# Folding the query weights in 32 by 32 array tiles, in two halves around the last key burst

## The chip, the cores and the metric

The kernel runs on one core of a Trainium2 chip. The metric is the device time of one execution in microseconds; the median of three runs of the kernel before is 507.56 us (507.46 to 507.66). Everything below comes from one further execution that was profiled.

## The reference

The kernel computes a gated mix of two branches over S = 2048 rows of width D = 512, all in float32:

```python
x = A_x
g = _sigmoid((x * gate_w).sum(-1, keepdims=True))
a = _A_ref(x, A_wqkv, A_w_phi, A_wo)      # linear attention, 32 heads of 16
b = _B_ref(x, B_w1, B_b1, B_w2, B_b2)     # relu(x @ w1 + b1)**2 @ w2 + b2, F = 1792
return g * a + (1 - g) * b
```

In branch A, `q`, `k` and `v` are `x @ wqkv`. Each head's `q` and `k` are multiplied by a 16 by 16 matrix (`w_phi`), and go through a softmax of both signs. The keys' features and `v` give a small matrix per head, `kv`, and a sum `z`; the queries' features are multiplied with them.

Since `q` is only ever used as `q @ w_phi`, the kernel multiplies the weights first: the query weights "folded" are `wq @ w_phi` head by head, a 512 by 512 matrix. This fold is what is changed here.

## The kernel before, in words

The contraction index of every product is cut into four chunks of 128 (`k` = 0 to 3), rows into blocks of 512, and the feed-forward width into 14 chunks. To keep float32 accuracy on TensorE, each operand is split into a high part (rounded, written by ScalarE: `activation ... Copy`, L63) and a low part (the rest, written by VectorE: a subtraction, L66), and a product is three matmuls (high by high, high by low, low by high: L76, L77, L78).

The program is one long list of work items. For each there is an `up` product (into a PSUM bank named `u`, read by ScalarE's ReLU at L421, then squared and split into `hh` and `hl`) and, two items later, a `down` product (into banks `d`). In this document u28, u29 and u30 are the up products with `w1` chunks 7, 8 and 9 around the change, one after the other. Attention work is hung between them at numbered slots by the calls of `at(slot, f)`; a scheduler then sets each engine's order by these and by priorities (`tc.high_priority`), and each engine runs its instructions strictly in the order built.

What lies around the change:

- The first seven chunks of the feed-forward run over all rows with the keys' and values' projections; the last key burst (`kvps`, L323) closes `kv`. VectorE then copies `kvps` out (L751), transposes it (L760) and writes `kvb` (L764), and SyncE writes `zrow` and loads `z` from it.
- The key weights are folded early, at 26 us, by `tiles_fold`: 64 matmul calls (128 records in the trace, two a call) of 32 by 32 weights and 128 columns, spread over all sixteen 32 by 32 tiles of the array and over four PSUM banks, with the roles of the operands swapped, so that VectorE's block transposition (L194) turns the result.
- The query weights are folded at slots 53 to 56 by `do_fold`: for each `k` four 128 by 128 products into one bank (`foldq`, L152), split into `wqh`, `wql` by ScalarE and VectorE straight from PSUM.
- At slot 56.5 the first projection of queries (`q`) needs all four `wqh`, `wql`.
- Three PSUM banks rotate at that time among `u`, `pY` and the folds (`bank`); a fourth joins with `kv_done`.
- Staging tiles `in` (four) hold loaded weights until they are split; a load waits until VectorE has split the tile's last content. `gated` (L445) adds a block's `d` banks into `row` tiles that ScalarE has filled (L893).

The program's functions that the change touches, with the line numbers of the profile:

Of the kernel before, what the change touches and what calls it, by code (L numbers as in the profile page):

```python
# [7 lines left out]
F32 = mybir.dt.float32  # L8
F32R = mybir.dt.float32r
# [6 lines left out]
P = 128  # L16
S, D, H, DH, F = 2048, 512, 32, 16, 1792
NK = D // P
# [10 lines left out]
AHEAD = 150  # L29
# [5 lines left out]
def tile_gated_mix(ctx: ExitStack, tc: tile.TileContext, xT, xn, wqT, wkT, wphi, wv, wo, w1, b1, w2, b2, gw, out):  # L35
    nc = tc.nc
# [4 lines left out]
    wpool = pool("wpool", 1)  # L41
    fpool = pool("fpool", NFH)
    work = pool("work", 2)
# [4 lines left out]
    banks = [ps_a, ps_b, ps_e, ps_f]  # L48
    def used(p):
        banks.remove(p)  # L50
        banks.append(p)

    def bank(name):
        p = banks[0]
        used(p)
        return p.tile([P, 512], F32, tag="s", name=name)
# [4 lines left out]
    def split(src, hi, lo, ehi, elo):  # L61
        if ehi is nc.scalar:
            i = nc.scalar.activation(hi, src, AF.Copy)  # L63
        else:
            i = ehi.tensor_copy(hi, src)
        st["lo"] = elo.tensor_tensor(lo, src, hi.bitcast(F32), ALU.subtract)  # L66
        return i
# [52 lines left out]
    st, up_w, down_w = {}, {}, {}  # L120
# [24 lines left out]
            nc.sync.dma_start(t[g + 1], wT[:, g, :])  # L145
        return t

    def fold(loaded, nm, k):
        wph, *t = loaded
        ps = bank(f"fold{nm}{k}")  # L150
        for g in range(NK):
            nc.tensor.matmul(ps[:, g * P:(g + 1) * P], t[g][:, k * P:(k + 1) * P], wph[:, g * P:(g + 1) * P],  # L152
                             start=True, stop=True)
        hi = wpool.tile([P, 512], F32R, tag=f"wah{k}", name=f"w{nm}h{k}")
        lo = wpool.tile([P, 512], F32R, tag=f"wal{k}", name=f"w{nm}l{k}")
        with tc.high_priority(offset=AHEAD):
            split(ps, hi, lo, nc.scalar, nc.vector)
        return hi, lo

    def both(t):  # L160
        return t[:, :512], t[:, 512:]

    def joint_start(loaded):
# [6 lines left out]
        for k in (0, 2, 1, 3):  # L170
            r = st["tmp"][k // 2] if k % 2 else work.tile([P, 2 * D], F32, tag="e", name=f"raw{k}", bufs=2)
            st["raw"][k] = r
            st["wv"] = nc.sync.dma_start(two(r)[:, :, 256:], two(wv[k * P:(k + 1) * P, :]))

    def tiles_fold(loaded):
        wph, *t = loaded
        pss = [bank(f"fold{r}") for r in range(4)]

        def mm(g, r, c):
            rows, cols = slice(32 * r, 32 * r + 32), slice(32 * c, 32 * c + 32)  # L180
            return nc.tensor.matmul(pss[r][cols, g * P:(g + 1) * P],
                                    wph[rows, g * P + 32 * r:g * P + 32 * r + 32],
                                    t[g][rows, :].rearrange("p (k c q) -> p k c q", c=4, q=32)[:, :, c, :],
                                    start=True, stop=True, skip_group_check=True)

        last = None
        for x in [(g, r, c) for g in range(NK) for c in range(4) for r in range(4)]:
            with tc.issue_after(last.ins) if last else nullcontext():
                last = mm(*x)
        for half in range(2):  # L190
            tb = work.tile([P, 2, 4, NK, 32], F32, tag="tb", name="turned", bufs=2)
            for r in range(2):
                with tc.high_priority(offset=AHEAD):
                    st["turned"] = nc.vector.transpose(tb[:, r].rearrange("p g k q -> p (g k q)"), pss[2 * half + r])  # L194
            for k in range(NK):
                dst = st["raw"][k].rearrange("p (h z g r f) -> p h z g r f", h=2, z=2, g=2, r=4)
                for h in range(2):
                    nc.scalar.activation(dst[:, h, 0, :, 2 * half:2 * half + 2],
                                         tb[:, :, 2 * h:2 * h + 2, k].rearrange("p r g q -> p g r q"), AF.Copy)

    def operand(i, j, src, slot=None, ehi=None, elo=None):
        if i in HELD:
# [116 lines left out]
    def kv_chunk(first, last, kvps, phi, v):  # L319
        for g in range(NG):  # L320
            for j in range(4):
                h = NG * j + g
                mm = nc.tensor.matmul(kvps[32 * j:32 * j + VW, 32 * g:32 * g + 32], v[:, h * VW:(h + 1) * VW],  # L323
                                      phi[:, 32 * h:32 * h + 32], start=(first and g == 0), stop=last,
                                      skip_group_check=True)
        return mm
# [129 lines left out]
    def do_wT(wT):  # L456
        st["wT"] = load_fold(wT)

    def do_fold(nm, k):
        with tc.issue_after(st["up"].ins):  # L460
            st["wa", nm, k] = fold(st["wT"], nm, k)
        if k == NK - 1:
            st["wa"] = [st["wa", nm, i] for i in range(NK)]
            if nm == "k":
                banks.pop()

    def do_joint(j, piece):
        if (j, piece) == (0, 0):
            joint_start(st["wT"])
            with tc.issue_after(st["up"].ins):  # L470
                tiles_fold(st["wT"])
        with tc.issue_after(st["up"].ins):
            joint(j, piece)
        if (j, piece) == (1, 0):
            banks.remove(ps_b)
# [121 lines left out]
    LASTP = len(ROWS) - 1  # L597
# [59 lines left out]
    def pair_steps(p, s):  # L657
        b, c = ROWS[p]
        n, m = b * NC + c, b * NC + c + 2
        v = {}  # L660
# [49 lines left out]
        def kv():  # L710
            if p == 0:
                st["kv"] = ps_b.tile([P, 2 * P], F32, tag="s", name="kvps")
            later = kv_chunk(p == 0, False, st["kv"], v["phi", m], v["v", m])
            with tc.issue_after(later.ins):
                kv_chunk(False, p == LASTP, st["kv"], v["phi", n], v["v", n])

        at(s - 2 - (p > 0), sums_load, p)
        if p == 0:
# [7 lines left out]
        at(s + 3, phi, n)  # L726
        at(s + 4, phi, m)
        at(s + 7.5 + (p == LASTP) / 2, kv)

    def do_q(b, n, c):  # L730
# [16 lines left out]
    def kv_done():  # L747
        kvps, kvs = st["kv"], st["kvs"]
        for j in range(4):
            s = slice(32 * j, 32 * j + VW)  # L750
            nc.vector.tensor_copy(kvs[s, :], kvps[s, :])  # L751
        nc.sync.dma_start(zrow.rearrange("(j x) -> j x", j=4), kvs[DH::32, :])
        for half in range(2):
            z = hold.tile([P, H * VW], F32, tag="vz", name=f"z{half}")[:, :D]
            nc.sync.dma_start(z, zrow[half * D:(half + 1) * D].partition_broadcast(P))
            zbc.append(z.rearrange("p (h f) -> p h f", f=DH))
        banks.append(ps_b)
# [27 lines left out]
    def at(slot, f, *a):  # L785
        steps.setdefault(int(2 * slot) / 2, []).append(lambda: f(*a))
# [10 lines left out]
    for b in range(NB):  # L797
        for c in range(NC):
            s = b * SL + 2.5 * c - 1 if b > 1 else 17.5 + c / 2 if b else max(5.5, 3.5 + 2 * c)
# [5 lines left out]
        s, late = ((4, 2), (19.5, 1), (22, 2.5), (36, 2))[b]  # L805
# [4 lines left out]
        pair_steps(p, 14 + 4.5 * p)  # L810
    base = (NB - 1) * SL
    at(49, do_wT, wqT)
    for k in range(NK):
        at(53 + k, do_fold, "q", k)
    for k in range(NK):
        at(base + 8.5 + k, wo_load, k)
        at(base + 10 + k, wo_split, k)
# [10 lines left out]
    for p in range(NB * NC // 2):  # L828
        n, s = 2 * p, 56.5 + 6 * p
        q, late = divmod(n, NC)[0], p == NB * NC // 2 - 1  # L830
# [13 lines left out]
    hid, last = {}, len(work_list) - 1  # L844
# [25 lines left out]
    for t, (sw, b, i) in enumerate(work_list):  # L870
# [17 lines left out]
        for c in range(NC):  # L888
            n = b * NC + c
# [62 lines left out]
```

## Time and profile before

| | |
|---|---|
| median of 3 runs | 507.56 us |
| the profiled execution, its time | 507.18 us |
| the profiled execution, first to last instruction | 505.4 us |
| TensorE busy | 500.7 us, 99% |
| VectorE busy | 407.0 us, 81% |
| ScalarE busy | 256.6 us, 51% |
| granted TensorE clock, mean | 0.999 of full |

The execution's time is 1.78 us longer than the span of its instructions. Matmuls overlap, so that each is listed longer than the distance to the next one; what a stretch of TensorE costs is read from start to start. In the timeline one row is one instruction or several alike, with their start, their duration and, in brackets, how long the engine was idle before and what released it.

### The profile page before, as it was taken

The numbers are of one execution on the slowest core, as the hardware profiler recorded it, in microseconds if no ns is written. First come the engines' busy times: TensorE is split into PE (matmuls) and PEld (weight loads), VectorE is DVE, ScalarE is ACT, GpSimd is POOL, SyncE is SP. The second block draws the span as 40 slices with busy tenths as digits, with TensorE's granted clock in tenths as the row PEclk, the third lists the DMA queues.
The fourth block names the chain that finished last, engine by engine and source line by source line (L and its number), as shares of the span: only waits on it lengthen the run. The fifth ranks groups of instructions, "written<-read, shape, count | busy, mean of one in ns | idle before, by whom it ended". The sixth has DMA issues, their size and how long they took to land.

```text
span 505.4 us, 9354 instructions
## 1 busy us (share of the span) xinstructions
PE 500.7 (99%) x3520; PEld 406.1 (80%) x3520; DVE 407.0 (81%) x680; ACT 256.6 (51%) x458; POOL 87.3 (17%) x102
## 2 busy tenths in 40 slices
PE   9999999999999999999999999999999999999997
PEld 5878888788888888888888878788787878788776
DVE  5569957988695979796998989897979796897724
ACT  4887655565253474454674744454455353333540
POOL 1000151204410035000013040212222221112200
PEclk9999999999999999999999999999999999999999
DMA  8858587756854578771265311325112231041112
GB/s 261 291 196 273 198 305 225 237 190 234 285 184 165 183 223 294 265 228 65 83 211 209 98 49 48 99 64 150 49 31 90 71 86 43 8 131 57 38 27 83
DMA packets 45829, 76.13 MB, mean 151 GB/s; under 512 B 6868, under 2 KB 23000, under 8 KB 45784
## 3 DMA queue, kind: packets, MB, share of 16 engines
q1 hardware_dynamic: 36072, 41.78, 26.6%
q10 hardware_dynamic: 6768, 23.79, 13.7%
q0 software_dynamic: 2944, 9.96, 5.5%
q8 instruction: 28, 0.46, 0.4%
q14 instruction: 17, 0.14, 0.1%
HBM read 57.68 MB, written 11.54 MB: 137 GB/s over the span
## 4 chain that ended last, share of the span: by engine, by line
PE 98%; DMA 1%; DVE 0%; issue 0%
PE d L76 10%; PE d L77 10%; PE d L78 10%; PE u L76 10%; PE u L77 9%; PE u L78 9%; PE pX L653 3%; PE q L77 3%; PE att L77 3%; PE att L78 3%; PE att L76 3%; PE q L78 3%; PE q L76 3%; PE pX L655 3%; PE pX L654 3%; PE pY L655 2%
## 5 line engine op out<-in xcount | busy, mean ns | idle before, releaser
L421 ACT ACTIVATE r<-u,b1c 128x512 f32<-128x512 f32 x56 | 38.5, 687 | 122.9 <-PE u L78 121.2
L76 PE MATMUL d<-w2h,hh 128*128 128x512 f32 x222 | 86.9, 391 | 0.0
L77 PE MATMUL d<-w2l,hh 128*128 128x512 f32 x222 | 86.4, 389 | 0.0
L78 PE MATMUL d<-w2h,hl 128*128 128x512 f32 x222 | 86.4, 389 | 0.0
L76 PE MATMUL u<-xh,w1h 128*128 128x512 f32 x212 | 83.6, 394 | 0.0
L77 PE MATMUL u<-xl,w1h 128*128 128x512 f32 x212 | 82.6, 390 | 0.0
L78 PE MATMUL u<-xh,w1l 128*128 128x512 f32 x212 | 82.5, 389 | 0.0
L333 POOL TENSOR_TENSOR ez<-e,z 128x512 f32<-128x512 f32 x32 | 42.9, 1360 | 165.0 <-ACT e L309 165.0
L66 DVE TENSOR_TENSOR hl<-r,hh 128x512 fp32r<-128x512 f32 x56 | 37.8, 676 | 24.3 <-ACT hh L63 24.1
L76 PEld LDWEIGHTS d<-w2h,hh 128*128 128x128 f32 x222 | 41.7, 188 | 9.2 <-issue 0.6
L76 PEld LDWEIGHTS u<-xh,w1h 128*128 128x128 f32 x212 | 39.8, 188 | 11.1 <-issue 2.9
L78 PEld LDWEIGHTS d<-w2h,hl 128*128 128x128 f32 x222 | 41.7, 188 | 8.7
L77 PEld LDWEIGHTS d<-w2l,hh 128*128 128x128 f32 x222 | 41.7, 188 | 8.5
L78 PEld LDWEIGHTS u<-xh,w1l 128*128 128x128 f32 x212 | 39.8, 188 | 8.6 <-DVE w1l L66 0.2
L77 PEld LDWEIGHTS u<-xl,w1h 128*128 128x128 f32 x212 | 39.8, 188 | 7.9
L309 ACT ACTIVATE e<-e 128x1024 f32<-128x1024 f32 x27 | 28.6, 1059 | 26.5 <-DVE e L307 26.1
L291 DVE TENSOR_REDUCE sm<-e 128x64 f32<-128x1024 f32 x27 | 32.8, 1215 | 10.8 <-ACT e L309 10.8
L63 ACT ACTIVATE hh<-r 128x512 fp32r<-128x512 f32 x56 | 35.2, 628 | 1.1
L423 ACT ACTIVATE r<-r 128x512 f32<-128x512 f32 x56 | 34.9, 624 | 0.7
L692 ACT ACTIVATE tmp<-pX 128x512 f32<-128x512 f32 x24 | 14.4, 598 | 30.6 <-PE pX L655 27.0
L374 ACT ACTIVATE phiT<-tb 32x256 f32<-32x256 f32 x64 | 26.4, 412 | 5.8 <-DVE tb L359 4.9
L343 DVE TENSOR_REDUCE dz<-ez 128x64 f32<-128x1024 f32 x16 | 19.4, 1212 | 11.7 <-POOL ez L333 11.7
(182 smaller groups left out, 984.2 us busy)
## 6 DMA issues: line engine op xcount, KB each, us to landing
sloto<-wkeep ACTq DMA_DIRECT2D x30, 512.0 KB, 4.6
in<-in_xT SPq DMA_DIRECT2D x42, 256.0 KB, 4.4
slotez<-wkeep ACTq DMA_DIRECT2D x15, 512.0 KB, 5.0
phiT<-tb SPq DMA_DIRECT2D x192, 32.0 KB, 1.8
in<-in_w SPq DMA_DIRECT2D x23, 256.0 KB, 3.3
part<-row POOLq DMA_DIRECT2D x16, 256.0 KB, 5.5
row<-part SPq DMA_DIRECT2D x16, 256.0 KB, 3.0
out<-row SPq DMA_DIRECT2D x15, 256.0 KB, 2.2
```

Of the source, the lines that this page charges most:

```text
L63: i = nc.scalar.activation(hi, src, AF.Copy)
L66: st["lo"] = elo.tensor_tensor(lo, src, hi.bitcast(F32), ALU.subtract)
L76: nc.tensor.matmul(o, ah[:, sa], bh[:, sb], start=first, stop=False)
L77: nc.tensor.matmul(o, ah[:, sa], bl[:, sb], start=False, stop=False)
L78: return nc.tensor.matmul(o, al[:, sa], bh[:, sb], start=False, stop=last)
L291: nc.vector.tensor_reduce(sm, e3, AX.X, ALU.add)
L309: nc.scalar.activation(ef, ef, AF.Exp)
L333: nc.gpsimd.tensor_tensor(ez[:, hs, :], e3[:, hs, :], zbc[half], ALU.mult)
L374: nc.scalar.activation(dst, src, AF.Copy)
L421: st["relu"] = nc.scalar.activation(r, ps, AF.Relu, bias=b1c[:, fc:fc + 1])
L423: nc.scalar.activation(r, r, AF.Square)
L655: nc.tensor.matmul(ps, l, wh, start=False, stop=j == 1, skip_group_check=True)
```

## The change

The query fold is done as the key fold was: 32 by 32 weights, operands swapped, results turned by VectorE's block transposition out of PSUM into an SBUF tile (`turned`), which is then split. It is done in two halves of 32 matmul calls each (64 products as the trace counts them, two records a call), each on eight array tiles (two row groups by four column groups) and two banks. The first half stands in the middle of u28, before the last key burst, the second in the middle of u29, behind it. Each half fills half of the columns of each `wqh[k]` and `wql[k]`, so there are eight narrower splits where there were four. The splits of the fold no longer have high priority; the transpositions and the copies out of `kvps` now have it.

```diff
-    def fold(loaded, nm, k):
-        wph, *t = loaded
-        ps = bank(f"fold{nm}{k}")
-        for g in range(NK):
-            nc.tensor.matmul(ps[:, g * P:(g + 1) * P], t[g][:, k * P:(k + 1) * P], wph[:, g * P:(g + 1) * P],
-                             start=True, stop=True)
-        hi = wpool.tile([P, 512], F32R, tag=f"wah{k}", name=f"w{nm}h{k}")
-        lo = wpool.tile([P, 512], F32R, tag=f"wal{k}", name=f"w{nm}l{k}")
-        with tc.high_priority(offset=AHEAD):
-            split(ps, hi, lo, nc.scalar, nc.vector)
-        return hi, lo
...
+    def fold_block(loaded, out, g, r, c):
+        wph, *t = loaded
+        rows, cols = slice(32 * r, 32 * r + 32), slice(32 * c, 32 * c + 32)
+        return nc.tensor.matmul(out[cols, g * P:(g + 1) * P], wph[rows, g * P + 32 * r:g * P + 32 * r + 32],
+                                t[g][rows, :].rearrange("p (k c q) -> p k c q", c=4, q=32)[:, :, c, :],
+                                start=True, stop=True, skip_group_check=True)
+
+    def turned(pss, half):
+        tb = work.tile([P, 2, 4, NK, 32], F32, tag="tb", name="turned", bufs=2)
+        for r in range(2):
+            with tc.high_priority(offset=AHEAD):
+                st["turned"] = nc.vector.transpose(tb[:, r].rearrange("p g k q -> p (g k q)"), pss[2 * half + r])
+        return tb
...
+    def query_fold(half):
+        pss = {r: bank(f"fold{r}") for r in (2 * half, 2 * half + 1)}
+        for g, c, r in [(g, c, r) for g in range(NK) for c in range(4) for r in pss]:
+            with tc.issue_after(st["up"].ins):
+                st["up"] = fold_block(st["wT"], pss[r], g, r, c)
+        tb = turned(pss, half)
+        part_ = lambda t: t.rearrange("p (g r f) -> p g r f", g=NK, f=32)[:, :, 2 * half:2 * half + 2, :]
+        for k in range(NK):
+            if not half:
+                st.setdefault("wa", []).append(tuple(
+                    wpool.tile([P, 512], F32R, tag=f"wa{hl}{k}", name=f"wq{hl}{k}") for hl in "hl"))
+            hi, lo = st["wa"][k]
+            split(tb[:, :, :, k].rearrange("p r g q -> p g r q"), part_(hi), part_(lo), nc.scalar, nc.vector)
...
-                kv_chunk(False, p == LASTP, st["kv"], v["phi", n], v["v", n])
+                st["up"] = kv_chunk(False, p == LASTP, st["kv"], v["phi", n], v["v", n])
...
-            nc.vector.tensor_copy(kvs[s, :], kvps[s, :])
+            with tc.high_priority(offset=AHEAD):
+                nc.vector.tensor_copy(kvs[s, :], kvps[s, :])
...
-    for k in range(NK):
-        at(53 + k, do_fold, "q", k)
+    at(52.5, query_fold, 0)
+    at(54.5, query_fold, 1)
```

`tiles_fold` (the key fold) now calls the same two helpers and computes in the same order as before.

The change also moves instructions on the other engines. On VectorE, between the end of the key burst and the first reduction over `q` (`mx`), the order before was (`wql` are the folded query weights' low parts, `row<-d` is `gated`):

```order
L66 TENSOR_TENSOR wol_2995<-in,woh_2994 128x512
L66 TENSOR_TENSOR w1l_3008<-in,w1h_3007 128x512
L66 TENSOR_TENSOR wql_3030<-foldq_3024,wqh_3029 128x512
L66 TENSOR_TENSOR hl<-r,hh 128x512
L66 TENSOR_TENSOR wol_3034<-in,woh_3033 128x512
L445 SCALAR_TENSOR_TENSOR row<-d_2348,rest,row 128x512
L66 TENSOR_TENSOR wql_3084<-foldq_3078,wqh_3083 128x512
L66 TENSOR_TENSOR w2l_3053<-in,w2h_3052 128x512
L445 SCALAR_TENSOR_TENSOR row<-d_2349,rest,row 128x512
L445 SCALAR_TENSOR_TENSOR row<-d_2350,rest,row 128x512
L445 SCALAR_TENSOR_TENSOR row<-d_2351,rest,row 128x512
```

The last low part stood behind one `gated` and ahead of the other three. The same place on VectorE now, from the second half's transpositions to the second half's four low parts:

```order
L174 STREAM_TRANSPOSE turned<-fold_3042 128x512
L174 STREAM_TRANSPOSE turned<-fold_3043 128x512
L66 TENSOR_TENSOR wol_3030<-in,woh_3029 128x512
L66 TENSOR_TENSOR w1l_3088<-in,w1h_3087 128x512
L449 SCALAR_TENSOR_TENSOR row<-d_2348,rest,row 128x512
L449 SCALAR_TENSOR_TENSOR row<-d_2349,rest,row 128x512
L449 SCALAR_TENSOR_TENSOR row<-d_2350,rest,row 128x512
L449 SCALAR_TENSOR_TENSOR row<-d_2351,rest,row 128x512
L66 TENSOR_TENSOR wql_2901<-turned,wqh_2900 128x4x64
L66 TENSOR_TENSOR wql_2905<-turned,wqh_2904 128x4x64
L66 TENSOR_TENSOR wql_2909<-turned,wqh_2908 128x4x64
L66 TENSOR_TENSOR wql_2913<-turned,wqh_2912 128x4x64
```

All four `gated` now stand ahead of the low parts, of which there are four narrow ones here; before, three of the four stood behind the last. Ahead of this piece stand, from the product of the last keys' features (`e<-e,r`) on: two transpositions of the first half, the gate's operations, `w2l`, `wol`, four narrow `wql`, `w1l`, four copies of `kvps`, `hl`, `wol`, `w2l`, the transposition and three of the four copies into `kvb`.

On ScalarE at the same place, before (`r<-u` is the ReLU of u29, `w1h<-in` the high part of a loaded `w1` chunk):

```order
L63 ACTIVATE w2h_2975<-in 128x512
L63 ACTIVATE wqh_2990<-foldq_2985 128x512
L63 ACTIVATE woh_2994<-in 128x512
L421 ACTIVATE r<-u,b1c 128x512
L63 ACTIVATE w1h_3007<-in 128x512
L63 ACTIVATE wqh_3029<-foldq_3024 128x512
```

The ReLU stood ahead of `w1h` and the block's fillings of `row` came later than all of these. On ScalarE at this place now:

```order
L63 ACTIVATE w2h_3019<-in 128x512
L890 ACTIVATE row<-b2b,rest 128x512 x2
L63 ACTIVATE woh_3029<-in 128x512
L63 ACTIVATE w1h_3087<-in 128x512
L890 ACTIVATE row<-b2b,rest 128x512 x2
L425 ACTIVATE r<-u,b1c 128x512
L63 ACTIVATE wqh_2900<-turned 128x4x64
```

The ReLU of u29 now stands behind `w1h` and the four fillings of `row`, and the second half's high parts behind it.

On TensorE at the first projection of queries, before, from the middle of u30:

```order
L78 MATMUL u<-xh_1_2061,w1l_2569 128x512
L76 MATMUL q_3096<-wqh_2890,xh_0_2037 128x512
L77 MATMUL q_3096<-wql_2891,xh_0_2037 128x512
L78 MATMUL q_3096<-wqh_2890,xl_0_2038 128x512
L76 MATMUL q_3096<-wqh_2990,xh_1_2061 128x512
```

The projection ran through from its first matmul. On TensorE at this place now:

```order
L78 MATMUL u<-xh_1_2061,w1l_2569 128x512
L76 MATMUL q_3158<-wqh_2900,xh_0_2037 128x512
L76 MATMUL u<-xh_2_2085,w1h_2568 128x512
L77 MATMUL u<-xl_2_2086,w1h_2568 128x512
L77 MATMUL q_3158<-wql_2901,xh_0_2037 128x512
```

Two matmuls of u30 have moved ahead of the first one that reads `wql`. u30 itself is computed into the bank that u29 used, before and now, so its first matmul waits for u29's ReLU.

## Rows read from the trace of the kernel before

**Rows 1.** The page: the chain that ended last, shares by engine.
```profile
PE 98%; DMA 1%; DVE 0%; issue 0%
```
**Rows 2.** Timeline of TensorE, 244 to 260 us: start, duration, line, names, count.
```profile
244.48 0.39 PE L78 MATMUL u<-xh,w1l 128*128 128x512 f32 x1
244.71 1.05 PE L152 MATMUL foldq<-row 128*128 128x128 f32 x8
...
245.83 0.40 PE L77 MATMUL d<-w2l,hh 128*128 128x512 f32 x1
...
257.03 1.05 PE L152 MATMUL foldq<-row 128*128 128x128 f32 x8
...
259.30 0.39 PE L76 MATMUL q<-wqh,xh 128*128 128x512 f32 x1
```
**Rows 3.** Timeline of TensorE at the key fold.
```profile
26.15 0.39 PE L78 MATMUL d<-w2h,hl 128*128 128x512 f32 x1
...
26.46 1.90 PE L181 MATMUL fold<-row 32*32 32x128 f32 x128
...
28.63 0.40 PE L77 MATMUL d<-w2l,hh 128*128 128x512 f32 x1
```
**Rows 4.** Timeline of TensorE at one numerator burst.
```profile
297.15 0.39 PE L78 MATMUL u<-xh,w1l 128*128 128x512 f32 x1
297.47 1.09 PE L385 MATMUL num<-phiT,kvb 64*32 64x256 f32 x32
...
298.83 0.40 PE L77 MATMUL u<-xl,w1h 128*128 128x512 f32 x1
```
**Rows 5.** Timeline of VectorE, 244 to 261 us.
```profile
244.99 1.21 DVE L314 TENSOR_TENSOR e<-e,r 128x1024 f32<-128x1024 f32 x1
246.12 0.69 DVE L266 SCALAR_TENSOR_TENSOR row<-row,gwb 128x512 f32<-128x512 f32 x1
...
246.73 0.68 DVE L66 TENSOR_TENSOR wql<-foldq,wqh 128x512 fp32r<-128x512 f32 x1
...
249.94 0.68 DVE L66 TENSOR_TENSOR wol<-in,woh 128x512 fp32r<-128x512 f32 x1
250.55 0.84 DVE L751 COPY row<-kvps 17x256 f32<-17x256 f32 x2
...
254.63 0.45 DVE L760 STREAM_TRANSPOSE row<-row 128x256 f32<-128x256 f32 x1
255.11 0.92 DVE L764 COPY kvb<-row 32x128 f32<-32x128 f32 x4
256.06 0.69 DVE L66 TENSOR_TENSOR wol<-in,woh 128x512 fp32r<-128x512 f32 x1
...
259.43 0.74 DVE L445 SCALAR_TENSOR_TENSOR row<-d,rest,row 128x512 f32<-128x512 f32 x1
260.10 0.68 DVE L66 TENSOR_TENSOR wql<-foldq,wqh 128x512 fp32r<-128x512 f32 x1
```
**Rows 6.** Timeline of VectorE at the key fold: the block transpositions out of PSUM.
```profile
28.35 2.51 DVE L194 STREAM_TRANSPOSE turned<-fold 128x512 f32<-128x512 f32 x4 [0.40 <-PE fold L181]
```
**Rows 7.** Timeline of VectorE, 236 us: an operation 256 wide, and the next.
```profile
236.27 0.41 DVE L674 TENSOR_TENSOR vext<-tmp,pY 128x256 f32<-128x256 f32 x1
236.60 0.68 DVE L304 TENSOR_REDUCE mx<-e 128x32 f32<-128x512 f32 x1
```
**Rows 8.** Timeline of ScalarE, 253 to 262 us.
```profile
253.99 0.67 ACT L421 ACTIVATE r<-u,b1c 128x512 f32<-128x512 f32 x1
255.89 0.63 ACT L63 ACTIVATE w1h<-in 128x512 fp32r<-128x512 f32 x1 [1.23 <-DMA in<-in_w]
...
260.23 1.94 ACT L893 ACTIVATE row<-b2b,rest 128x512 f32<-128x512 f32 x3
```
**Rows 9.** Timeline of SyncE's DMA queue: the issue of that `w1` load.
```profile
251.93 0.36 SPq L86 DMA_DIRECT2D in<-in_w  x1
```
**Rows 10.** Timeline of TensorE, first microseconds: the warm-up matmuls of 512 columns.
```profile
1.19 4.45 PE L497 MATMUL warm<-zeros 128*128 128x512 bf16 x10 [1.19 <-DVE zeros L491]
```

More of the change, by code (lines that the diff above doesn't have):

```diff
@@ L173, in joint_start @@
             st["wv"] = nc.sync.dma_start(two(r)[:, :, 256:], two(wv[k * P:(k + 1) * P, :]))
-    def tiles_fold(loaded):
[L176 to L184, printed above, removed]
+    def fold_block(loaded, out, g, r, c):
[10 more added lines that the diff above has]
+        return tb
+    def tiles_fold(loaded):
+        pss = {r: bank(f"fold{r}") for r in range(4)}
         last = None
-        for x in [(g, r, c) for g in range(NK) for c in range(4) for r in range(4)]:
+        for g, c, r in [(g, c, r) for g in range(NK) for c in range(4) for r in range(4)]:
             with tc.issue_after(last.ins) if last else nullcontext():
-                last = mm(*x)
+                last = fold_block(loaded, pss[r], g, r, c)
         for half in range(2):
[L191 to L194, printed above, removed]
+            tb = turned(pss, half)
             for k in range(NK):
@@ L199, in tiles_fold @@
                                          tb[:, :, 2 * h:2 * h + 2, k].rearrange("p r g q -> p g r q"), AF.Copy)
+    def query_fold(half):
[3 more added lines that the diff above has]
+                st["up"] = fold_block(st["wT"], pss[r], g, r, c)
+        tb = turned(pss, half)
+        part_ = lambda t: t.rearrange("p (g r f) -> p g r f", g=NK, f=32)[:, :, 2 * half:2 * half + 2, :]
[5 more added lines that the diff above has]
+            split(tb[:, :, :, k].rearrange("p r g q -> p g r q"), part_(hi), part_(lo), nc.scalar, nc.vector)
     def operand(i, j, src, slot=None, ehi=None, elo=None):
@@ L457, in do_wT @@
         st["wT"] = load_fold(wT)
[L459 to L465, printed above, removed]
     def do_joint(j, piece):
```

## The prediction

> **What bounds the kernel now.** I read the chain of waits first: it is TensorE for 98% of the span [rows 1], so what counts is what TensorE executes and where it is made to wait. Next came the timeline of TensorE around the query folds, 244 to 260 us [rows 2], where the reader should see that nothing there waits: each row starts where the one ahead allows. Then I read the queues of VectorE [rows 5] and ScalarE [rows 8] in the same stretch, since the changed fold passes through both of them before the queries' first projection, and there the reader should see how full VectorE is.
>
> **What TensorE saves.** From the last u28 matmul at 244.48 to the second `d` matmul at 245.83 are 1.35 us, in which two ordinary steps and one fold lie. An ordinary step from one 512-column matmul to the next is 0.23 us (244.48 to 244.71). So a fold costs 1.35 - 0.46 = 0.89 us, and the four of them, the last at 257.03, 3.56 us [rows 2].
>
> The new half, 64 records of 128 columns on eight tiles, does not stand in the trace. Two rows are near. The key fold is 128 such records on sixteen tiles: 26.15 to 28.63 is 2.48, less two steps 2.02 us [rows 3]. The numerator burst has eight tiles in the same shape of two row groups by four column groups, 32 records of 256 columns, as many columns in all as a half: 297.15 to 298.83 is 1.68, less two steps 1.22 us [rows 4]. A half therefore lies between 1.0 (half the key fold) and 2.0 us (no faster for having half the records); I take 1.22, the row with the same tiles and columns. Two halves cost 2.44 us and TensorE saves 1.1 us. Without any wait it would reach the first matmul of `q` at 259.30 - 1.1 = 258.2, and the first one that reads `wql`, three steps later, at 258.9.
>
> **What VectorE adds, and where it stands.** The order on each engine is known. On VectorE it is unchanged up to the product `e<-e,r`, which starts at 244.99 with the engine busy from there on [rows 5]. I add up what is queued from there to the first low part of the second half, `wql`, which that matmul of `q` reads, from start to start:
>
> - the product itself 1.13 (244.99 to 246.12) and the gate's multiplication 0.61 (to 246.73) [rows 5];
> - two transpositions of the first half: four took 2.51 us, so 1.25 [rows 6];
> - `w2l`, `wol`, `w1l`, `hl` and three small gate operations: the stretch 246.73 to 249.94 holds these and one more low part, 3.21 us; a low part is 0.61 (249.94 to 250.55), which leaves 2.60 [rows 5];
> - four narrow `wql` of the first half: an operation 256 wide takes 0.33 to the next start, so 1.32 [rows 7];
> - four copies of `kvps` at 0.42, 1.68; then `hl`, `wol`, `w2l` and, further on, `wol`, `w1l`: the first three and the last two are five, of which one is the `hl` already counted, so four at 0.61, 2.44 [rows 5];
> - the transposition of `kv` 0.48 (254.63 to 255.11) and three of the four copies into `kvb`, 0.71 of 0.95 [rows 5];
> - two transpositions of the second half 1.25 [rows 6];
> - four `gated` at 0.67 (259.43 to 260.10), 2.68 [rows 5];
> - and the low part itself, 0.41 from start to end [rows 7].
>
> The sum is 16.6 us, so it is ready at 261.56. TensorE wanted it at 258.9 and is late by 2.7 us. Before, the last of the four wide low parts started at 260.10 [rows 5] and was done ahead of TensorE, with one `gated` in front of it in place of four; the other three `gated` came behind. What the change puts in front of that low part is three more `gated`, 2.0 us, and four transpositions, 2.5 us. The other three narrow parts follow every 0.33 us, faster than the 0.68 us in which `q` uses up one chunk, so the wait comes once.
>
> The narrow low part (4 by 64, out of SBUF, into every other block of 64) is the operation that the trace doesn't show. It can't well be quicker than a copy 128 wide, 0.23 from 255.11 on, nor slower than a full one, 0.61 [rows 5]. Five stand in the sum, so its bounds are 0.6 us less and 1.3 us more; I take the row of its own width.
>
> Nothing on VectorE in this stretch should wait for another engine. The second half's products end near 252.7, its transpositions start near 256.0. The closest is `w1l` near 257.8, for which the `w1` chunk must be loaded: its load was issued at 251.93 and ready at 255.89, 3.96 us [rows 8, 9]; now its staging tile comes free when `w1l` of the first half's stretch ends, near 251.4, and the issue lies near 252.4 behind the same `wo` load, so that it arrives near 256.4, is split high by 257.0, and holds VectorE up only if it is 0.8 us later.
>
> **The second new wait, on ScalarE.** The ReLU of u29 ran at 253.99, ahead of that `w1h` [rows 8]. Now it is behind it and behind two of the fillings of `row`: 257.0, two at 0.65 (three took 1.94), then the ReLU with 0.67, done near 259.0 [rows 8]. u30 writes the bank that this ReLU frees. TensorE wants to start u30 six steps ahead of `q`, at 256.8, and stands until 259.0, 2.2 us. It then reaches the reader of `wql` after six steps of u30 and three more, at 261.0, and waits another 0.5 us for VectorE. The two waits overlap: the end is VectorE's 261.56.
>
> **The sum.** -1.1 us of TensorE's work, +2.7 us of waiting: +1.6 us. The profiled execution would go from 507.18 to 508.8 and its span from 505.4 to 507.0; the median shown is 0.4 us above the profiled execution, and from it, 507.56, I forecast 509.1 us. Since the chain is TensorE's, the loss is not given back later: after `q` the order on TensorE is as before. The earlier copies of `kvps` and loads of `z` serve readers behind `q` and gain nothing. A half's cost between 1.0 and 2.0 us changes nothing either, as TensorE would arrive between 258.4 and 260.4, ahead of 261.56.
>
> [...]
>
> **The rivals.**
>
> *It is faster.* If VectorE had `wql` ready by 258.9 and ScalarE the ReLU by 256.8, only TensorE's 1.1 us would be left: 506.4 us. For it speaks that TensorE never waited here before; against it that the decisive point, 2.7 us less on VectorE, is just the four `gated` that the order puts in front. 6%. [...]
>
> *VectorE's queue is shorter than I add up.* With narrow low parts near 0.23 us the wait is 2.1 us, and with a little less elsewhere the whole lands between 508.0 and 508.5. 12%.
>
> *The load decides.* If the `w1` chunk arrives 0.6 us or more later than in the row, ScalarE's path passes VectorE's, and each further microsecond of it is one of TensorE's: at 1.5 us late, 510.1. SyncE issues it in another neighbourhood now, so this can be. 14%.
>
> *The clock falls.* TensorE would stand still for over 2 us, which it never does in the trace. [...] 5%.
>
> **How the numbers follow.** The forecast has 63%, with a range of its own from 508.5 to 510.0. Differences under 0.2%, 1.0 us, can't be told from none. Slower by more: the forecast, the load and the clock, 82%. Within: the shorter queue, 12%. Faster: 6%. The range that should hold the time 8 times in 10 goes from 508.2 to 510.6: it leaves out the gain, the clock and the ends of the others.
>
> **What the changed profile would show.** Each half some 1.2 us on TensorE; the narrow `wql` near 0.33 us apart; four `gated` ahead of the last four `wql`; TensorE idle for about 2.2 us ahead of u30, released by the ReLU, and for about 0.5 us ahead of `q` at the first `wql`, released by VectorE; the ReLU of u29 behind a `w1h` that waited for its load. I am wrong if TensorE shows no idle time there, or if VectorE's queue reaches that `wql` well before 261 us.

## The result, and the profile after

The changed kernel takes 509.25 us (median of 11 runs, 508.49 to 511.14) beside 507.56 us for the kernel before on the same chip (11 runs, 506.95 to 508.05): 1.0041 times as long, 95% interval 1.0028 to 1.0054. Run a second time, beside other runs of the kernel before, it took 1.0045 times as long (1.0029 to 1.0062). It is slower, by 1.7 us. Its profiled execution took 509.01 us with a span of 507.2.

The view of what TensorE waits for (us in total, times, longest) had nothing in this stretch before; of the kernel after it says:

```profile
PE q L77 <- DVE wql L66: 1.5, 1, 1.5
...
PE u L76 <- ACT r L425: 0.7, 1, 0.7
```

These are the two waits that were foretold, the long one at the second half's first `wql`, the other at the bank that the ReLU frees. The timeline of TensorE after, beside [rows 2]:

```profile
251.32 0.39 PE L78 MATMUL u<-xh,w1l 128*128 128x512 f32 x1
251.63 1.15 PE L166 MATMUL fold<-row 32*32 32x128 f32 x64
...
253.06 0.40 PE L77 MATMUL u<-xl,w1h 128*128 128x512 f32 x1
...
256.70 0.39 PE L78 MATMUL d<-w2h,hl 128*128 128x512 f32 x1
257.82 0.50 PE L76 MATMUL u<-xh,w1h 128*128 128x512 f32 x1 [0.73 <-ACT r L425]
...
259.77 0.39 PE L77 MATMUL u<-xl,w1h 128*128 128x512 f32 x1
261.67 0.50 PE L77 MATMUL q<-wql,xh 128*128 128x512 f32 x1 [1.52 <-DVE wql L66]
```

The reader should take the waits from start to start: 256.70 to 257.82 is 1.12, less an ordinary step of 0.23 it is 0.89; 259.77 to 261.67 is 1.90, less 0.23 it is 1.67. The half burst with the matmul behind it runs from 251.63 to 253.06; the matmul ahead of it started at 251.32, so it costs 1.74 - 0.46 = 1.28 us. The other half, at 243.43, gives the same 1.28.

VectorE after, beside [rows 5 to 7]:

```profile
256.01 1.31 DVE L174 STREAM_TRANSPOSE turned<-fold 128x512 f32<-128x512 f32 x2
...
258.57 2.72 DVE L449 SCALAR_TENSOR_TENSOR row<-d,rest,row 128x512 f32<-128x512 f32 x4
261.20 1.42 DVE L66 TENSOR_TENSOR wql<-turned,wqh 128x256 fp32r<-128x256 f32 x4
```

The four `gated` stand ahead of the `wql`, no idle time is shown anywhere between the second half's transpositions and these, and the first `wql` starts at 261.20: with 0.40 us it is done at 261.60, and TensorE starts at 261.67. ScalarE after, beside [rows 8]:

```profile
255.36 0.61 ACT L63 ACTIVATE w1h<-in 128x512 fp32r<-128x512 f32 x1
255.88 1.32 ACT L890 ACTIVATE row<-b2b,rest 128x512 f32<-128x512 f32 x2
257.11 0.66 ACT L425 ACTIVATE r<-u,b1c 128x512 f32<-128x512 f32 x1
```

The ReLU stands behind `w1h` and two fillings, as foretold, but `w1h` no longer waits for its load and the whole row is 1.2 us earlier than forecast. SyncE had issued that load 0.28 us earlier than before, not later [rows 9]:

```profile
251.65 0.36 SPq L86 DMA_DIRECT2D in<-in_w  x1
```

### The profile page after: what moved, and what is told of

It is laid out like the page before. It is cut to its first block, busy times and chain, and to the rows that moved or that the text cites. A ratio compares the mean times of both kernels' runs of the same rounds, so it can differ in the third digit from the quotient of the medians.

```text
span 507.2 us, 9563 instructions
## 1 busy us (share of the span) xinstructions
PE 500.5 (99%) x3616; PEld 404.4 (80%) x3616; DVE 408.1 (80%) x688; ACT 257.3 (51%) x462; POOL 87.3 (17%) x102
## 4 chain that ended last, share of the span: by engine, by line
PE 98%; DVE 1%; issue 0%; DVEq 0%
PE d L76 10%; PE d L77 10%; PE d L78 10%; PE u L76 10%; PE u L78 9%; PE u L77 9%; PE pX L649 3%; PE q L77 3%; PE pX L651 3%; PE pX L650 3%; PE att L76 3%; PE q L78 3%; PE att L78 3%; PE att L77 3%; PE q L76 3%; PE pY L650 2%
```

## The experiments

Theory: VectorE's queue ahead of the second half's `wql` sets the end, and ScalarE's late ReLU is a second wait that lies beneath it. Rivals: the ReLU alone; the small tiles themselves (bursts and transpositions); the clock. Each kernel ran beside the kernel before, whose median was 507.77 us with the first four experiments, 507.31 with the second four and 507.43 with the last four. Against which line of the changed kernel each edit goes is said by its diff.

**relu_first.** The ReLU goes ahead of the fillings.

```
+                with tc.issue_after(st["relu"].ins) if b == NB - 1 else nullcontext():
                     nc.scalar.activation(o, b2b, AF.Copy, scale=rest[:, n:n + 1])
```

> The four fillings of `row` in the last block are issued behind the ReLU of u29; nothing else is edited. On ScalarE the ReLU then stands directly behind `w1h`, on VectorE the four `gated`, which read those fillings, fall behind the four low parts `wql` of the second half. Theory (VectorE's queue ahead of that `wql` sets the end, ScalarE's late ReLU overlaps with it): in the changed kernel the first `wql` starts at 261.20 behind four `gated` of 2.72 us; without them it starts near 258.5 and is done near 258.9, while TensorE, no longer held at u30 (0.89 us from start to start), wants it near 259.1. Both waits go, 0.89 + 1.67 us: 506.7 to 507.1 us, which is below the 507.56 of the kernel before. Rival 1 (ScalarE alone): only the wait at u30 goes, 508.4. Rival 2 (the bursts or their switching cost the time, not the waits): 509.2, unchanged.

Measured: 507.81 us, 0.9998 times before (0.9986 to 1.001). Its timeline of TensorE:

```profile
258.62 0.39 PE L76 MATMUL q<-wqh,xh 128*128 128x512 f32 x1
258.97 0.50 PE L77 MATMUL q<-wql,xh 128*128 128x512 f32 x1
...
297.31 0.62 PE L389 MATMUL num<-phiT,kvb 64*32 64x256 f32 x2
298.13 1.09 PE L389 MATMUL num<-phiT,kvb 64*32 64x256 f32 x30 [0.21 <-DMA phiT<-tb]
299.15 0.50 PE L76 MATMUL u<-xh,w1h 128*128 128x512 f32 x1
```

Both waits are gone (0.12 us is left between 258.62 and 258.97), and `q` starts 0.7 us ahead of 259.30 [rows 2]. Rivals 1 and 2 fall. But the time is 0.7 us above the range that the theory expected: a new wait stands at the first numerator burst (the packed products `num` of the queries' features with `kvb`), where two records run at 297.31 and the others at 298.13. What the burst reads comes from VectorE, from the first `q` (`mx`) over the transposition `tb`. The timeline of VectorE in the kernel before:

```profile
252.28 0.69 DVE L66 TENSOR_TENSOR w2l<-in,w2h 128x512 fp32r<-128x512 f32 x1 [0.89 <-ACT w2h L63]
...
263.27 0.68 DVE L304 TENSOR_REDUCE mx<-q 128x32 f32<-128x512 f32 x1
...
285.15 1.24 DVE L359 STREAM_TRANSPOSE tb<-e 128x1024 f32<-128x1024 f32 x1
```

The same places in relu_first, with its `wql` ahead of them:

```profile
245.32 1.21 DVE L318 TENSOR_TENSOR e<-e,r 128x1024 f32<-128x1024 f32 x1
...
258.49 1.43 DVE L66 TENSOR_TENSOR wql<-turned,wqh 128x256 fp32r<-128x256 f32 x4
...
264.88 0.68 DVE L308 TENSOR_REDUCE mx<-q 128x32 f32<-128x512 f32 x1
...
286.63 1.24 DVE L363 STREAM_TRANSPOSE tb<-e 128x1024 f32<-128x1024 f32 x1
```

VectorE is 1.6 us late at `mx` and still 1.5 us late 22 us further on. Of both, 0.33 us are not the edit's: this whole execution already ran that much later ahead of the change (`e<-e,r` at 245.32, 244.99 in [rows 5]). Less that, `q` is 1.0 us early, which is TensorE's whole saving; VectorE is 1.3 us late at `mx` and 1.15 us at `tb`; TensorE reaches the burst 0.5 us early and leaves it 0.3 us late (299.15, 298.50 before). The transpositions added 2.5 us to VectorE, but came to only 1.3 us at `mx`, in part because VectorE before had a break of 0.89 us, for `w2h`, in this stretch, and has none here.

**low_first.** The splits of the query fold get priority.

```
+            with tc.high_priority(offset=AHEAD):
                 split(tb[:, :, :, k].rearrange("p r g q -> p g r q"), part_(hi), part_(lo), nc.scalar, nc.vector)
```

> Only the splits of the query fold get priority: on VectorE the four `wql` of the second half stand ahead of all four `gated`, but on ScalarE the ReLU of u29 stands behind the four `wqh` of that half too. Theory (two waits that overlap, each able to set the end): VectorE's wait goes, ScalarE's grows. The transpositions of the second half end near 257.4, four `wqh` at 0.33 us bring ScalarE to 258.7, the ReLU with 0.66 us to 259.4; u30 wants to start at 256.9 and stands 2.4 us, against 0.89 + 1.67 = 2.56 us in the changed kernel: 509.1 us, with the one wait in place of the two. Rival 1 (VectorE's four `gated` alone): 1.67 us less or more, 507.6 at most, 506.7 if u30 waits no longer. Rival 2 (ScalarE's ReLU alone, VectorE's wait separate from it): u30's wait grows by 1.5 us on top, 510.8.

Measured: 510.84 us, 1.0061 (1.0047 to 1.0075). Its timeline of TensorE:

```profile
257.23 0.39 PE L78 MATMUL d<-w2h,hl 128*128 128x512 f32 x1
259.89 0.50 PE L76 MATMUL u<-xh,w1h 128*128 128x512 f32 x1 [2.28 <-ACT r L426]
...
261.97 0.63 PE L76 MATMUL q<-wqh,xh 128*128 128x512 f32 x1
262.39 0.63 PE L77 MATMUL q<-wql,xh 128*128 128x512 f32 x1
```

One wait of 2.43 us (257.23 to 259.89, less 0.23) in place of two, released by the ReLU, and none at `wql`: as the theory has it. Nearly all of the 1.7 us above its 509.1 is the clock, not rival 2's larger wait: after the wait matmuls start 0.43 us apart (262.39 - 261.97), and eight steps from 260.69 to 264.10 take 3.41 us in place of 1.82, 1.6 us more. In this profile's table by windows:

```profile
260.00:262.00 2.00, 2.00 (x7) 1.57 (x8) 2.00 (x5) 1.97 (x4) 0.48 (x1) 0.67 0.80 191
262.00:264.00 2.00, 2.00 (x6) 1.61 (x5) 2.00 (x4) 0.21 (x1) 1.67 (x4) 0.50 0.88 249
264.00:266.00 2.00, 2.00 (x10) 1.58 (x10) 1.09 (x3) 0.00 (x0) 0.03 (x1) 0.98 1.03 383
```

(window, its length, busy us and instructions of PE, PEld, DVE, ACT and POOL, the granted clock, DMA share, GB/s). The granted clock is 0.50 from 262 to 264 us; it was 1.00 from 250 to 260 us and is 1.00 again from 266 to 270. Its mean was 0.997 in five of the six runs. The one run at 1.0 took 510.12 us, 1.0 us above the theory's time, so that the profile bears the theory out and this single time does not; runs of the kernel before lay between 506.57 and 510.05 us beside it.

**relu_first_low_last.** As relu_first, with the second half's splits in a step of their own (slot 56), behind the last `gated`. Of the edit only this is shown:

```
...
+            with tc.issue_after(st["gated"].ins) if half else nullcontext():
                 split(tb[:, :, :, k].rearrange("p r g q -> p g r q"), part_(hi), part_(lo), nc.scalar, nc.vector)
```

> The fillings of `row` stand behind the ReLU of u29 as in relu_first, but the second half's splits are held behind the last `gated`. TensorE's wait at u30 is gone, VectorE's queue is not shortened: all four `gated`, and now `hl`, `wol` and `w2l` too (three at 0.61 us), stand ahead of the first `wql`. Theory (VectorE sets the end): that `wql` is done 1.8 us later than the 261.6 of the changed kernel, near 263.4; on TensorE five more steps of 0.23 us, 1.1 us, stand ahead of the matmul that reads it, so the end moves by some +0.6: 509.9 us, with one TensorE wait of some 3 us, released by VectorE at `wql`. Rival (ScalarE's late ReLU is what costs): the ReLU is as early as in relu_first, so 0.9 us is gained, 508.4 or, where the wait at `wql` goes as well, 506.7.

Measured: 513.31 us, 1.0108 (1.009 to 1.0126). The ReLU's rival expected a gain and falls, but the experiment is not clean: the edit held `wqh` on ScalarE too, TensorE stood for that one (1.60 us, released by ScalarE) more than for `wql` (0.30), and 2.1 us more at the first numerator burst, behind which the granted clock was 0.50 from 304 to 306 us. I rest nothing else on it.

**old_fold_low_last.** The kernel before, its splits without priority.

```
-        with tc.high_priority(offset=AHEAD):
-            split(ps, hi, lo, nc.scalar, nc.vector)
+        split(ps, hi, lo, nc.scalar, nc.vector)
```

> The kernel before, with its four old folds of 0.89 us, but with their splits not given priority: on VectorE all four `gated`, and `hl`, `wol`, `w2l`, stand ahead of the last `wql`; on ScalarE the four fillings of `row` stand ahead of its `wqh`. Theory (the place in VectorE's queue costs the time, not the small tiles): the last `wql` is done near 263.7 (from `w1l` at 256.7: 0.61, three copies 0.7, a low part 0.6, three more 1.8, four `gated` 2.7, itself 0.6) where TensorE, with four steps moved ahead of it, wants it near 262.5; 1.2 us lost: 508.7 us without any small tile. Rival (the small tiles and their transpositions are what costs): 507.5 us as before.

Measured: 508.42 us, 1.0014 (1.0004 to 1.0024). Its timeline of TensorE at the last `wql`:

```profile
263.09 0.39 PE L76 MATMUL u<-xh,w1h 128*128 128x512 f32 x1
263.71 0.50 PE L77 MATMUL q<-wql,xh 128*128 128x512 f32 x1 [0.23 <-DVE wql L66]
```

Its timeline of VectorE, what stands ahead of that `wql`:

```profile
245.83 1.21 DVE L313 TENSOR_TENSOR e<-e,r 128x1024 f32<-128x1024 f32 x1
...
260.34 2.72 DVE L444 SCALAR_TENSOR_TENSOR row<-d,rest,row 128x512 f32<-128x512 f32 x4
262.98 0.68 DVE L66 TENSOR_TENSOR wql<-foldq,wqh 128x512 fp32r<-128x512 f32 x1
```

The same wait appears without a small tile, once the four `gated` stand ahead of a `wql`. Its sign is as expected, its size 0.4 us (263.09 to 263.71, less 0.23) in place of 1.2. Both engines ran 0.84 us later here from ahead of the folds on (`e<-e,r` at 245.83, 244.99 in [rows 5]; the last fold at 257.88, 257.03 before), which changes nothing between them. Less that, TensorE wants the `wql` at 262.5, as expected, but VectorE has it done at 262.8, not 263.7: the expectation added three copies into `kvb` (0.7 us) behind `w1l` without taking them out ahead of it, and VectorE's break for `w2h` was 0.61 us in place of 0.89.

**relu_first_copies_on_scalar and relu_first_kvb_on_scalar.** On top of relu_first, relieve VectorE: is it VectorE's fullness that makes the numerator burst late? The second has only the lower edit.

```
-                nc.vector.tensor_copy(kvs[s, :], kvps[s, :])
+                nc.scalar.activation(kvs[s, :], kvps[s, :], AF.Copy)
...
-            nc.vector.tensor_copy(kvb[s, :, DH * (j % 2):DH * (j % 2 + 1)], kt[s, :, :DH])
+            nc.scalar.activation(kvb[s, :, DH * (j % 2):DH * (j % 2 + 1)], kt[s, :, :DH], AF.Copy)
```

> relu_first, and in addition the four copies out of `kvps` (0.42 us each) and the four into `kvb` (0.23 us each) run on ScalarE; VectorE loses 2.6 us ahead of the first `mx` of q, TensorE's order stays. In the profile of relu_first both waits around u30 and `q` were gone (0.12 us left), but TensorE stood 0.84 us at the first numerator burst: VectorE ran `mx` at 264.88 (263.27 in the kernel before) and, busy without a break, carried that 1.5 us on to the transposition `tb`, 286.63 against 285.15, whose product the burst reads. Theory (VectorE's 2.7 us of added work is carried to that burst): the wait there goes, 507.81 - 0.84 = 507.0 us. Rival 1 (the burst waits for the transfers themselves, not for VectorE): no change, 507.8. Rival 2 (ScalarE now is the late engine): 2.6 us of copies stand ahead of the ReLU of u29 there, u30 waits again and the time is 508.3 or more.

> relu_first with only the four copies into `kvb` on ScalarE: 0.92 us less on VectorE. Theory (VectorE's carried lateness): 0.92 us is just more than the 0.84 us that the burst waited, so the wait there is 0 to 0.1 and the time 507.0 us. Rival 1 (transfers): 507.8. Rival 2 (ScalarE late): 0.92 us ahead of the ReLU of u29, at most 0.5 us of wait at u30, 507.5.

Measured: 507.47 us, 1.0001 (0.9992 to 1.001), and 508.07 us, 1.0016 (1.0007 to 1.0025). Neither gained what was expected. The timeline of VectorE in the first of them:

```profile
255.98 0.69 DVE L66 TENSOR_TENSOR wol<-in,woh 128x512 fp32r<-128x512 f32 x1 [1.99 <-ACT woh L63]
...
260.44 0.75 DVE L449 SCALAR_TENSOR_TENSOR row<-d,rest,row 128x512 f32<-128x512 f32 x1 [0.62 <-ACT row L891]
...
264.88 0.68 DVE L308 TENSOR_REDUCE mx<-q 128x32 f32<-128x512 f32 x1
```

The 2.6 us saved on VectorE became 2.6 us of waiting for ScalarE, which now was the late one; `mx` starts at the same 264.88 and the burst waits as long. In the other, TensorE stood 0.93 us at u30 for the ReLU behind the copies. So the theory was not tested as meant, though both fit the 12.52 us at the end of this section. One premise of it is also not so: VectorE is not busy without a break from `mx` to `tb`. In the kernel before and in relu_first it stands 1.4 us there for GpSimd's `ez`, so that what hands the lateness on is the chain behind `mx`, on several engines, and not VectorE's work alone.

**before_copies_on_scalar.** The same two edits in the kernel before.

> The kernel before with the same eight copies on ScalarE. Theory: TensorE waited for nothing there, so 2.6 us less on VectorE is worth nothing: 507.5 to 507.8 us. Rival (moving the copies is a gain by itself, and relu_first_copies_on_scalar shows only that): about as much less here as there, 507.0.

Measured: 507.21 us, 0.9999 (0.9988 to 1.001). Nothing to gain, as expected.

**changed_again.** The changed kernel, no edit.

> The changed kernel once more, beside the others on the same chip. Theory: 509.2 us, two TensorE waits of 0.9 and 1.7 us; the granted clock falls in some of its runs only (it was 0.996 in three of eleven, at 510.8 to 511.1 us, where low_first, standing 2.3 us in one piece, had 0.997 in five of six and old_fold_low_last, standing 1.3 us, in none of twelve). Rival (the clock's fall is part of what the change costs in every run): the mean granted clock is below 1.0 in most runs.

Measured: 509.88 us, 1.0045 (1.0029 to 1.0062). The profiled run, at 510.93, caught what the first profile didn't. Its timeline of TensorE:

```profile
262.00 0.50 PE L77 MATMUL q<-wql,xh 128*128 128x512 f32 x1 [1.83 <-DVE wql L66]
...
262.84 0.63 PE L77 MATMUL q<-wql,xh 128*128 128x512 f32 x1
263.27 0.63 PE L78 MATMUL q<-wqh,xl 128*128 128x512 f32 x1
```

Its table by windows, the granted clock third from the end:

```profile
263.00:264.00 1.00, 1.00 (x4) 0.81 (x3) 1.00 (x2) 0.00 (x0) 0.00 (x0) 0.50 1.08 428
...
266.00:267.00 1.00, 1.00 (x6) 0.81 (x5) 0.58 (x1) 0.00 (x0) 0.00 (x0) 0.92 0.48 119
```

The two waits are 0.56 and 1.99 us here (257.03 to 257.82 and 259.78 to 262.00, less 0.23 each), in sum the 2.55 us that they were in the first profile, 2.56. Behind the wait at `wql` the clock is at half for 3.4 us, with matmuls 0.43 us apart (263.27 - 262.84), which costs 1.6 us. The mean granted clock was 0.996 in four of the changed kernel's sixteen runs, which took 510.8 to 511.1 us, and 0.999 or 1.0 in the others (508.5 to 509.9). In the 72 runs of the kernel before that stood beside the experiments it was never below 0.999. So the fall is not a part of every run: in this profile it stands behind the wait of 1.99 us, and in the first profile, with 1.67 us there, the granted clock is 1.00 from 250 to 270 us. (The 1.3 us that the expectation gives old_fold_low_last are a misreading; its profile shows the 0.4 us above.)

**fills_on_gpsimd.** The cleaner form of relu_first_low_last: ScalarE is rid of the fillings, VectorE's order stays.

```
-                nc.scalar.activation(o, b2b, AF.Copy, scale=rest[:, n:n + 1])
+                if b == NB - 1:
+                    nc.gpsimd.tensor_scalar(o, b2b, rest[:, n:n + 1], None, ALU.mult)
+                else:
+                    nc.scalar.activation(o, b2b, AF.Copy, scale=rest[:, n:n + 1])
```

> The changed kernel with the last block's four fillings of `row` on GpSimd and nothing else: ScalarE's ReLU of u29 stands directly behind `w1h`, VectorE's order stays (four `gated` ahead of the second half's `wql`; three copies into `kvb` fall behind). Theory (VectorE's queue sets the end, ScalarE's wait lies beneath it): no wait at u30; the first `wql` near 260.9 (261.6 less 0.7) where TensorE, which now reads it two steps earlier, wants it near 258.6: one wait of some 2.2 us and 508.9 us in runs at full clock, up to 1.6 us more where the granted clock falls behind it. Rival (the late ReLU is the cause): u30's 0.9 us is gained and the wait at `wql` doesn't grow, 508.3 or less.

Measured: 510.63 us, 1.0049 (1.0032 to 1.0067). Its timeline of TensorE:

```profile
258.68 0.39 PE L76 MATMUL q<-wqh,xh 128*128 128x512 f32 x1
261.26 0.54 PE L77 MATMUL q<-wql,xh 128*128 128x512 f32 x1 [2.19 <-DVE wql L66]
```

Its timeline of VectorE:

```profile
258.16 2.72 DVE L449 SCALAR_TENSOR_TENSOR row<-d,rest,row 128x512 f32<-128x512 f32 x4
260.79 1.42 DVE L66 TENSOR_TENSOR wql<-turned,wqh 128x256 fp32r<-128x256 f32 x4
```

No wait at u30, one of 2.35 us at `wql`: taking ScalarE's wait away lengthened VectorE's, as it must where two waits overlap. In six of seven runs the mean granted clock was 0.996 or 0.997 (509.9 to 510.9 us). In the profiled one, at 0.997, eight steps from 261.60 to 265.00 take 3.40 us in place of 1.82, 1.6 us more; less that, the median of the six is 509.1. The one run at 0.999 took 508.37, nearer to the rival's time, so that it is the profile, not the time, that decides here.

**fills_on_gpsimd_low_first and fills_on_gpsimd_light_vector.** On top of that edit, the splits of both halves get priority, the second half's in a step of their own (slot 55) behind the ReLU; the second kernel also has the copies out of `kvps` on ScalarE.

```
...
+            with tc.high_priority(offset=AHEAD), tc.issue_after(st["relu"].ins) if half else nullcontext():
                 split(tb[:, :, :, k].rearrange("p r g q -> p g r q"), part_(hi), part_(lo), nc.scalar, nc.vector)
```

> The changed kernel with the last block's four fillings of `row` on GpSimd, and the second half's splits a step of their own with priority, behind the ReLU of u29. So the ReLU stands early on ScalarE and the four `wql` stand ahead of the four `gated` on VectorE, but VectorE has the same work ahead of the first `mx` of q as in relu_first, less one copy of 0.23 us. In relu_first_copies_on_scalar VectorE stood 2.0 us for ScalarE and 0.6 us for a filling of `row`, so it reached `mx` at the same 264.88 in spite of 2.6 us less work, and the theory of a full VectorE was not tested. Theory (VectorE's added 2.7 us is carried to the first numerator burst): waits at u30 and `wql` of 0.2 us at most, `mx` near 264.7, and a wait of 0.6 to 0.8 us at that burst: 507.6 to 507.8 us. Rival (the late fillings of `row`, not VectorE's work, made that burst late): `mx` near 263, no wait at the burst, 507.0.

> fills_on_gpsimd_low_first, with the four copies out of `kvps` on ScalarE: 1.7 us less on VectorE, nothing between them that waits for ScalarE's copies. Theory (VectorE full): `mx` near 263.0, as early as in the kernel before (263.27), no wait at the numerator burst: TensorE's saving of about 1.0 us is left, less 0.2: some 0.7 us below the kernel before, near 506.8. Rival (the burst waits for something else): a wait of 0.6 us or more stays, 507.6 or more.

Measured: 510.04 us, 1.0046 (1.0033 to 1.0059), and 507.88 us, 1.0008 (0.9996 to 1.0019): both miss. The timeline of VectorE in the second:

```profile
252.70 0.95 DVE L66 TENSOR_TENSOR w2l<-in,w2h 128x512 fp32r<-128x512 f32 x1
...
254.04 2.25 DVE L767 COPY kvb<-row 32x128 f32<-32x128 f32 x4
...
264.65 0.69 DVE L314 TENSOR_REDUCE mx<-q 128x32 f32<-128x512 f32 x1
```

While GpSimd filled the rows, from 252.23 on for 6.39 us, the four copies into `kvb` took 2.25 us where they took 0.92 [rows 5], and VectorE reached `mx` 1.4 us later than in the kernel before, though it was rid of 1.7 us of copies. ScalarE's `w1h` waited for its load until 256.45, and u30 stood 0.94 us. In the first of the two TensorE stood 0.64, 0.43 and 0.99 us around `q`.

**before_fills_and_copies.** The kernel before with fillings on GpSimd and the copies out of `kvps` on ScalarE.

> The kernel before with the two edits of fills_on_gpsimd_light_vector: fillings on GpSimd, copies out of `kvps` on ScalarE. Theory: TensorE waited for nothing there, nothing to gain: 507.3 to 507.7 us. Rival (those two edits are the gain, not the small tiles): as much below the kernel before as fills_on_gpsimd_light_vector.

Measured: 512.64 us, 1.0096 (1.0074 to 1.0117): no control, but the theory once more. GpSimd was late (its fillings began at 257.31), each `gated` waited for one, and the last `wql` stood behind them, in the timeline of VectorE:

```profile
263.54 0.75 DVE L445 SCALAR_TENSOR_TENSOR row<-d,rest,row 128x512 f32<-128x512 f32 x1 [0.79 <-POOL row L894]
264.21 0.68 DVE L66 TENSOR_TENSOR wql<-foldq,wqh 128x512 fp32r<-128x512 f32 x1
```

TensorE waited 3.6 us for that `wql` (261.13 to 264.95, less 0.23), with the old fold, and the mean granted clock was 0.993 or 0.997 in five of the six runs. The rival, that these edits are a gain by themselves, falls.

**What the seven profiles say together of the numerator burst.** From the start of `tb` on VectorE to the first matmul behind the burst are 12.52 us in relu_first (286.63 to 299.15), and 12.52, 12.52, 12.51 and 12.51 in the four other kernels where the burst ran late (relu_first_copies_on_scalar, relu_first_kvb_on_scalar, fills_on_gpsimd_light_vector, fills_on_gpsimd_low_first), though TensorE reached the burst between 297.28 and 299.05. In the kernel before it is 13.35 (285.15 to 298.50) and in the changed one 13.36 (286.99 to 300.35), of which these are the rows:

```profile
286.99 1.24 DVE L363 STREAM_TRANSPOSE tb<-e 128x1024 f32<-128x1024 f32 x1
```

```profile
299.32 1.09 PE L389 MATMUL num<-phiT,kvb 64*32 64x256 f32 x32
300.35 0.50 PE L76 MATMUL u<-xh,w1h 128*128 128x512 f32 x1
```

So this path has 0.83 us to spare before, and VectorE's lateness beyond that is paid in full. In the changed kernel it stays hidden only because TensorE is itself 1.85 us late by then.

## Why the prediction was right, point by point

- *TensorE saves 1.1 us.* A half costs 1.28 in place of 1.22; saved are 3.56 - 2.56 = 1.0 us.
- *VectorE's queue, 16.6 us from 244.99.* Summed to 261.56, measured 261.60. [rows 5] leave out that VectorE before was not busy throughout: it stood 0.89 us at 251.39 for `w2h`. The sum rightly has no such break, since the added work fills it. The narrow low parts are the 0.33 to 0.34 us that were taken from the row of their own width, so the shorter queue, a rival, did not occur.
- *ScalarE's wait.* This term was mis-sized. It rested on the `w1` load arriving near 256.4, from an issue near 252.4 behind a load of `wo`; SyncE was done with those loads at 251.53, the issue lies at 251.65, and `w1h` runs at 255.36 without waiting. The ReLU is done at 257.77, not near 259.0, and u30 waits 0.89, not 2.2 us. Since the two waits overlap, VectorE's grew from the forecast 0.5 to 1.67 and the end did not move: the forecast had taken the later of the two as the end, so this is not luck. low_first and fills_on_gpsimd show that exchange from either side.
- *The sum.* +2.7 - 1.1 = +1.6 was forecast. Measured: +0.89 + 1.67 of waits, 0.11 each for the matmul behind a wait (0.34 in place of 0.23 to the next start), less 1.0: +1.8, which is the difference of the spans, 507.2 - 505.4. TensorE saved 0.1 us less than forecast, 0.2 us of restarts were missing in the sum, and the waits were 0.14 us shorter; that these errors cancel in part is luck. Nothing is given back later, as forecast: at the first numerator burst, 299.32 against 297.47, it is still 1.85.
- *The faster case* asked for 2.7 us less on VectorE, namely without the four `gated`. relu_first gave that order, and no gain: the condition was stated too narrowly. VectorE's added work, four transpositions of 2.5 us of which 1.3 us are left at `mx`, makes the next reader late, the numerator burst, whose margin is 0.83 us. That the transpositions alone do this is argued from these sums and not shown: each experiment that was to relieve VectorE ran into ScalarE or GpSimd instead. The forecast said that the wait comes once; with the `wql` early it would come there.
- *The load* did not decide: in the changed kernel `w1h` did not wait for it. In fills_on_gpsimd_light_vector it did, and u30 stood 0.94 us, but the numerator burst had the last word there too.
- *The clock* was given 5% and fell in four of sixteen runs, to a mean of 0.996; in the profile of changed_again that costs 1.6 us, behind a wait of 1.99 us. The runs that it hit lie above the range, the rest inside.

## What to carry to other kernels

Saving on the engine that sets the time is worth only what the next engine has to spare: add up the queue of the engine that takes over the work, to every later reader and not only to the first. Two waits that overlap are told apart by removing one and watching the other grow, not by the time. A wait on TensorE can cost more than itself: here the granted clock was 0.50 behind waits of 1.99 us (changed_again) and 2.43 us (low_first), which cost 1.6 us more each time.

No version run here is faster than the kernel before; relu_first is level with it. That VectorE's added work alone, put into the kernel before at the same place, would cost as much was not tried.

## What the runs showed of the hardware

- After TensorE had stood 1.99 us at `wql` and 0.56 a little ahead (changed_again), and after 2.43 us (low_first, mean 0.997 in five of six runs), the granted clock was 0.50, and matmuls started 0.43 us apart in place of 0.23. After 2.35 us (fills_on_gpsimd, mean 0.996 or 0.997 in six of seven runs) they started as far apart. In each of these profiles this lasted 3.4 us and cost 1.6 us.
- Beside the fillings on GpSimd, VectorE's four copies into `kvb`, 32 partitions by 128, took 0.56 us each in place of 0.23, and the low part `w2l` 0.95 in place of 0.69 (fills_on_gpsimd_light_vector); `w1l` and `w2l` took 1.02 and 1.09 in fills_on_gpsimd_low_first. The transpositions out of PSUM kept their 1.31 us for two in both. Not every low part was slower beside the fillings: `hl` and `wol` took 0.68 in fills_on_gpsimd_low_first, and in fills_on_gpsimd none from 253.41 us on took over 0.74, while the four fillings took 7.09 us there and 6.19 in before_fills_and_copies. What decides which operations are slower was not shown.
- Four fillings of 128x512 took 6.19 us on GpSimd in before_fills_and_copies, 1.55 each; on ScalarE three took 1.94 [rows 8], 0.65 each.
